# Cosine attention with a GELU layer: in batches 3 to 7, a score chunk issued in halves beside the values, sums of the third group later, and new run lengths

## The chip, the core and the metric

The kernel runs on one core of a Trainium2 chip. The metric is device time in microseconds (us): 401.73, the median of 3 runs (401.44 to 402.19). All other times come from one profiled execution; they are counted from the start of its span. Engines: TensorE (PE in the profile, PEld its weight loads), VectorE (DVE), ScalarE (ACT), GpSimd (POOL), and SP, which only issues transfers.

## The reference, cut to what matters

```python
# q, k, v: (8, 12, 448, 64); tau = 0.1; w_in: (768, 2048); w_out: (2048, 768)
q_n = q / (norm(q, axis=-1) + 1e-6);  k_n = k / (norm(k, axis=-1) + 1e-6)
attn = softmax(q_n @ k_n.T / tau)            # for each of 8 batches and 12 heads
x = (attn @ v) as (8 * 448, 12 * 64)         # heads side by side
out = gelu(x @ w_in) @ w_out                 # gelu with erf
```

The scores of normalised rows are at most 10, and the kernel leaves the maximum out of its softmax.

## The kernel before, in words

**Groups and chunks.** The 12 heads of a batch are three groups of four heads; there are 24 groups, `g0 = 3 * b` being a batch's first. A group's 448 keys are seven chunks of 64. `scores` (L232) computes one chunk for four heads as four 64x64 matmuls of 448 columns (a *quad* here): two on rows 0 to 63 of the array (s = 0), two on rows 64 to 127 (s = 1). The result fills a pair of PSUM banks; `exps` (L246) turns the pair into bf16 `pt` with one exp of 896 columns on ScalarE. `visit(p, ...)` (L647) does this for the next chunks in order, one for each number given, and the number says which of three bank pairs is used. The counter `at` runs ahead of the batch: the chunks that are scored in batch b >= 3 belong to a later group than the one whose values are taken.

**Values.** `values` (L317) multiplies a group's seven chunks by v, a quad each, into one more pair, `o`. `spread` (L355) lays out one over the softmax's sums, and `normalise` (L360) multiplies `o` by it into `x`, both on VectorE, twice a group. `weighted` (L371) is values, spread where that has not been done, and normalise.

**Sums.** From batch 3 on, the softmax's sums are not made by TensorE. A group's `pt` chunks are added up by GpSimd (`folded`, L258: the second and third group of a batch) or by VectorE (`gathered`, L265: the first). `turned_all` (L272) and `inverted_all` (L285) then reduce and invert them on VectorE (L276, L278, L281, L290, L294).

**Norms.** q and k are squared (L158), reduced (L168), and the root of each norm is taken by Ln and Exp on ScalarE (`norms`: L175, L180) and inverted on VectorE (`inverted_norms`: L186, L188). GpSimd scales q and k (L204), and SP's transfers transpose them (L216) for the scores.

**The two layers.** `first(b)` (L821) is x times w_in, 16 tiles `hp` of six matmuls each (L462), and GELU on ScalarE (L887). Four matmuls of each of the first six tiles come first, then the last two, which need the third group's part of `x`. The second layer, g times w_out (L399), is cut into *pieces* of 16 matmuls, each in one bank, which VectorE copies out (L403). The pieces of the batch before are the `fill` of `attention(b)`: 96 matmuls (batches 3, 5, 7) or 128 (batches 4, 6), which `run()` hands out in the lengths of `parts`, between the stretches of scores and values. So in batches 3 to 7 TensorE alternates between runs of op matmuls and stretches of quads.

**Banks.** Pieces and odd hp tiles share two banks, `mm0` and `mm1`; `mm_tile` takes the one whose turn it is and flips the turn. With `aside=0` it takes that bank and leaves the turn. Three more pairs serve scores, `o`, hp pairs (the dictionary `pairs` in `first`) and `gathered`.

**What sets the order.** The schedule is manual: each engine executes in the order in which the code issues, and waits for another engine where data or a buffer ask for it. VectorE's order therefore is the code's: a copy of a piece is issued with the piece's last matmul, and stands behind whatever was issued on VectorE before.

In batches 3 to 7 (the last branch of `attention`) the order before is: run, 3 visits around the first group's values, run, 3 visits, run, 3 visits around the second group's values, run, 3 visits, run, 3 visits with the norms and `turned_all` of the third group, run, the inversions, 3 visits, two runs, and 3 visits around the third group's values. In batch 7 only the chunks that are still left are scored.

```python
# L102 to L106
    def mm_tile(name, shape=(128, 512), dtype=F32, aside=None):
        t = ps_mm.tile(list(shape), dtype, tag=f"mm{turn[0] if aside is None else turn[0] ^ aside}", name=name)
        if aside is None:
            turn[0] ^= 1
        return t
```

Of the kernel before, what the change touches and what calls it, by code (L numbers as in the profile page):

```python
# [10 lines left out]
BF16 = mybir.dt.bfloat16  # L11
# [5 lines left out]
def kernel(  # L17
# [17 lines left out]
    nc = tc.nc  # L35
# [262 lines left out]
    def sums(g, chunks=range(C)):  # L298
        for c in chunks:
            if c == 0:  # L300
                bank_t[g, "sm"] = ps_acc.tile([128, 512], F32, tag="sm", name=f"sm{g}") if g < NQ else \
                    mm_tile(f"sm{g}", aside=0)
            for s in range(2):
                if g < NQ:
                    nc.tensor.matmul(bank_t[g, "sm"][64 * s:64 * (s + 1), :S],  # L305
                                     lhsT=ones2.rearrange("p a h r -> p (a h r)"), rhs=pt_t[g, s, c],
                                     start=(c == 0), stop=(c == C - 1), tile_position=(0, 64 * s))
                    continue

                half = 2  # L310
                for i in range(2) if c == half else ((c - (c > half)) % 2,):
                    r = 32 * (2 * s + i)
                    cols = slice(i * S // 2, (i + 1) * S // 2) if c == half else slice(0, S)
                    nc.tensor.matmul(bank_t[g, "sm"][r:r + 32, cols], lhsT=ones, rhs=pt_t[g, s, c][:, cols],  # L314
                                     start=(c < 2), stop=(c >= C - 2), tile_position=(0, r))

    def values(g, chunks=range(C), p=None):  # L317
        for c in chunks:
# [13 lines left out]
    rs_t = {}  # L332
# [314 lines left out]
    def visit(*pairs):  # L647
        for p in pairs:
            g, c = divmod(at[0], C)
            at[0] += 1  # L650
            if g < NG:
                scores(g, ((0, c), (1, c)), p)
                exps(g, ((0, c), (1, c)))

    def attention(b, fill):
        fill = list(fill)
        if b == 1:
            parts = iter((20, 13, 14, 17, 16, 16))
        elif b == 2:
            parts = iter((22, 12, 12, 13, 11, 13, 11, 11, 11, 6, 6))  # L660
        elif len(fill) == 128:
            parts = iter((20, 18, 18, 18, 18, 18, 9, 9))
        else:
            parts = iter((14, 13, 14, 14, 14, 13, 7, 7))

        def run(n=None):
            for _ in range(next(parts) if n is None else n):
                fill.pop(0)()

        def norms(n):  # L670
            if n < len(groups):
                logs(n)
                roots(n)
                done[root] = n + 1

        def inverted_norms(n):
            if n < len(groups):
                inverses(n)

        def squared(n, i):  # L680
            if n < NU:
                square(n, ((nc.scalar, i),))
                done[square] = n + 1

        def reduced(n, i):
            if n < NU:
                reduce(n, i)
                done[reduce] = n + 1

        x_t[b] = xp.tile([128, KD, S], BF16, tag="x", name=f"x{b}")  # L690
        g0, u = b * NQ, b * NQ + 1
        run()
        if b == 1:
            upto(scale, u + 3)
            upto(load_v, b + 2)
            upto(transposes, u + 3)
            upto(load_qk, g0 + NQ + 2)
            upto(square, u + 4)
            visit(0, 1, 2)
            run()  # L700
            visit(0, 1, 2)
            run()
            upto(load_qk, g0 + NQ + 3)
            visit(0, 1)
            upto(square, u + 5)
            run()
            visit(0, 1, 2)
            both(g0, 0)
            upto(load_v, b + 3)
            upto(load_qk, g0 + NQ + 4)  # L710
            visit(1, 2)
            upto(reduce, u + 4)
            run()
            visit(1, 2, 0)
            both(g0 + 1, 1)
            visit(2, 0)
            logs(6)
            roots(6)
            run()
            both(g0 + 2, 2)  # L720
            inverses(6)
            done[root] = 7
        elif b == 2:
            upto(scale, u + 3)
            upto(load_qk, g0 + 6)
            upto(transposes, u + 3)
            upto(scale, u + 4)
            upto(load_qk, g0 + 7)
            upto(transposes, u + 4)
            visit(0, 1, 2)  # L730
            run()
            visit(0, 1, 2)
            norms(9)
            inverted_norms(9)
            upto(scale, u + 5)
            upto(transposes, u + 5)
            upto(load_qk, g0 + 9)
            upto(square, u + 6)
            run()
            visit(1, 2)  # L740
            total(g0)
            weighted(g0, 0)
            visit(1, 2)
            squared(u + 6, 0)
            run()
            visit(1, 2, 0)
            run()
            reduced(u + 5, 0)
            visit(1, 2)
            squared(u + 6, 1)  # L750
            total(g0 + 1)
            weighted(g0 + 1, 0)
            visit(1, 2)
            reduced(u + 5, 1)
            folded(g0 + 2, range(C - 1))
            run()
            for i in range(2):
                reduced(u + 6, i)
            visit(1, 2, 0)
            folded(g0 + 2, range(C - 1, C))  # L760
            upto(load_v, b + 3)
            run()
            visit(1, 2, 0)
            run()
            visit(1, 2, 0)
            run()
            visit(1, 2, 0)
            norms(10)
            run()
            turned_all(g0 + 2)  # L770
            run()
            inverted_norms(10)
            inverted_all(g0 + 2)
            visit(1, 2)
            weighted(g0 + 2, 0)
            visit(1)
        else:
            upto(scale, u + 5)
            upto(transposes, u + 5)
            upto(load_qk, g0 + 9)  # L780
            visit(1, 2)
            weighted(g0, 0)
            visit(1)
            reduced(u + 5, 0)
            squared(u + 6, 0)
            folded(g0 + 2, range(3))
            run()
            reduced(u + 5, 1)
            visit(2, 1, 0)
            folded(g0 + 2, range(3, 6))  # L790
            run()
            reduced(u + 6, 0)
            for h in range(2):
                spread(g0 + 1, h)
            visit(2, 0)
            weighted(g0 + 1, 1)
            visit(2)
            squared(u + 6, 1)
            folded(g0 + 2, range(6, 7))
            upto(load_v, b + 3)  # L800
            run()
            visit(0, 2, 1)
            run()
            reduced(u + 6, 1)
            visit(0, 2, 1)
            norms(2 * b + 6)
            turned_all(g0 + 2)
            run()
            inverted_norms(2 * b + 6)
            inverted_all(g0 + 2)  # L810
            visit(0, 2, 1)
            run()
            run()
            for h in range(2):
                spread(g0 + 2, h)
            visit(1, 2)
            weighted(g0 + 2, 0)
            visit(1)
        assert not fill, len(fill)

    def first(b):  # L821
# [3 lines left out]
        nc.scalar.preload_act_table_set(GELU_SET)  # L825
        u = (b + 1) * NQ + 1
        hps = dict(early) if b == 0 else {}
        pairs = ({0: 1, 2: 0, 6: 1, 8: 0}, {2: 0, 4: 1, 6: 2, 8: 0}, {2: 2, 4: 1, 8: 2})[min(b, 2)]
        ahead = 6 if b else 5

        def mm(m, kds):
# [6 lines left out]
            elif m not in hps:  # L838
                hps[m] = mm_tile(f"hp{b}_{m}")[:, :S]

        for m in (0, 2, 3, 4, 5, 1) if b > 1 else range(ahead):
            bank(m)
            mm(m, range(2 if b == 0 and m in early else 0, KD - 2))
        if b == 0:
# [5 lines left out]
        elif b == 1:  # L850
            upto(scale, u + 1)
            upto(transposes, u + 1)
            upto(load_qk, (b + 1) * NQ + 5)
            upto(square, u + 3)
            upto(reduce, u + 2)
        elif b + 1 < B:
            for n in range(3, 5):
                upto(scale, u + n)
                upto(transposes, u + n)
                upto(load_qk, (b + 1) * NQ + 4 + n)  # L860
            folded((b + 1) * NQ + 1)
            if u + 4 < NU:
                square(u + 4, ((nc.scalar, 0), (nc.scalar, 1)))
            if u + 5 < NU:
                square(u + 5, ((nc.scalar, 0),))
            upto(reduce, u + 5)
            gathered((b + 1) * NQ, 0)
            turned_all((b + 1) * NQ)
            inverted_all((b + 1) * NQ)
            spread((b + 1) * NQ, 0)  # L870
            spread((b + 1) * NQ, 1)
            turned_all((b + 1) * NQ + 1)
            inverted_all((b + 1) * NQ + 1)
            done[square] = u + 6
# [94 lines left out]
```

## Time and profile before

| | |
|---|---|
| median of 3 runs | 401.73 us (401.44 to 402.19) |
| the profiled execution | 401.45 us, of which the span is 399.6 |
| granted TensorE clock | 1.000 |
| busy: PE, DVE, ACT, POOL | 98%, 66%, 67%, 63% of the span |
| hp matmuls L462 | 768, 147.0 us busy |
| op matmuls L399 | 864, 148.9 us busy |
| score matmuls L242 | 672, 49.5 us busy |
| value matmuls L328 | 672, 36.9 us busy |
| first hp matmul of batches 3, 4, 5, 6, 7 | 176.72, 225.24, 268.56, 317.08, 357.05 |
| exp over 896 columns L252 | 168, mean 916 ns |
| GELU over 448 columns L887 | 128, mean 552 ns |

How to read it: a line of the timeline gives start, length, engine, source line, operation, output and inputs, shapes, and how many instructions were merged; in square brackets stand the idle time before it and what ended that. Matmuls are pipelined, so their durations overlap, and the pace is read from their starts. An engine's idle time costs nothing unless TensorE waits for it in turn.

### The profile page before, as it was taken

How to read it: one execution, taken by the hardware profiler on the slowest of the kernel's cores; microseconds unless marked ns; L12 is line 12 of the kernel's file. 1: busy time of each engine (PE TensorE's matmuls, PEld its weight loads, DVE VectorE, ACT ScalarE, POOL GpSimd, SP SyncE). 2: the span in 40 equal slices, each digit the busy share in tenths (PEclk: the TensorE clock that was granted, in tenths of full speed). 3: DMA queues.
4: the chain of work that ended last, by engine and by line, in shares of the span. 5: the costliest groups of instructions: out<-in, count | busy, mean ns of one | idle time of the engine just before them, and what ended most of it. 6: DMA issues, size and time to landing. Idle time of an engine off the chain costs nothing.

```text
span 399.6 us, 8019 instructions
## 1 busy us (share of the span) xinstructions
PE 393.0 (98%) x3245; PEld 205.6 (51%) x3245; DVE 262.0 (66%) x530; ACT 266.9 (67%) x386; POOL 250.6 (63%) x162
## 2 busy tenths in 40 slices
PE   7999999999999999999999999999999999999996
PEld 3444555555545555555555555555555555555564
DVE  5787214955487999679976599679975695470021
ACT  6995787557998877797576867788656746504300
POOL 5898804269699694969495981969677760910000
PEclk9999999999999999999999999999999999999999
DMA  8999999847296890679066770665032700130033
GB/s 289 260 258 216 203 220 303 176 105 222 52 263 221 160 227 2 181 126 275 21 116 153 174 204 0 178 111 133 2 85 52 171 14 2 41 79 2 0 81 80
DMA packets 66485, 54.52 MB, mean 136 GB/s; under 512 B 38672, under 2 KB 62352, under 8 KB 66448
## 3 DMA queue, kind: packets, MB, share of 16 engines
q1 hardware_dynamic: 54464, 41.79, 39.5%
q0 software_dynamic: 11600, 11.80, 18.7%
q8 instruction: 25, 0.41, 0.4%
q10 hardware_dynamic: 384, 0.43, 0.4%
q14 instruction: 12, 0.10, 0.1%
HBM read 45.61 MB, written 11.01 MB: 142 GB/s over the span
## 4 chain that ended last, share of the span: by engine, by line
PE 95%; DMA 2%; SPq 1%; DVE 1%; ACT 1%; issue 0%; ACTq 0%
PE hp L462 37%; PE op L399 36%; PE st L242 10%; PE o L328 8%; DMA qk<-in_k_dram 2%; PE op L418 1%; PE sm L305 1%; PE sm L314 1%; PE tp L221 1%; SPq L133 1%; ACT sq L158 0%; PE spin L456 0%; ACT pt L252 0%; DVE tr L336 0%; DVE rs L357 0%
## 5 line engine op out<-in xcount | busy, mean ns | idle before, releaser
L252 ACT ACTIVATE pt<-st 128x896 bf16<-128x896 f32 x168 | 143.1, 916 | 37.0 <-PE st L242 36.5
L399 PE MATMUL op<-wo,g 128*128 128x384 bf16 x864 | 148.9, 327 | 0.0
L462 PE MATMUL hp<-x,wi 128*128 128x448 bf16 x768 | 147.0, 353 | 0.1
L204 POOL TENSOR_TENSOR qkb<-qk,rn 128x896 bf16<-128x896 f32 (+1 forms) x50 | 80.3, 1628 | 62.5 <-DVE rn L188 61.1
L399 PEld LDWEIGHTS <-g 128*128 128x128 bf16 x864 | 81.0, 98 | 64.7 <-issue 14.1
L462 PEld LDWEIGHTS <-wi 128*128 128x128 bf16 x768 | 74.4, 98 | 71.5 <-issue 3.1
L887 ACT ACTIVATE g<-hp 128x448 bf16<-128x448 f32 x128 | 63.6, 552 | 66.9 <-PE hp L462 66.7
L263 POOL TENSOR_TENSOR acc<-acc,pt 128x896 f32<-128x896 f32 x55 | 103.8, 1886 | 4.3
L403 DVE COPY ot<-op 128x384 f32<-128x384 f32 x54 | 29.6, 548 | 78.1 <-PE op L399 75.7
L168 DVE TENSOR_REDUCE nq<-sq 128x14 f32<-128x896 f32 (+1 forms) x50 | 50.9, 1038 | 12.8 <-POOL sq L160 6.7
L242 PE MATMUL st<-qkT 64*64 64x448 bf16 x672 | 49.5, 358 | 0.2 <-ACT pt L252 0.2
L160 POOL TENSOR_TENSOR sq<-qk 128x896 f32<-128x896 f32 x18 | 29.9, 1683 | 16.3 <-DMA qk<-in_q_dram 11.9
L328 PE MATMUL o<-pt,v 64*64 64x448 bf16 x672 | 36.9, 350 | 0.3 <-DVE x L362 0.3
L270 DVE TENSOR_TENSOR acc<-acc,pt 128x896 f32<-128x896 f32 x30 | 33.0, 1099 | 1.0
L362 DVE TENSOR_TENSOR x<-o,rs 128x448 bf16<-128x448 f32 x48 | 27.5, 608 | 9.1 <-PE o L328 8.8
L158 ACT ACTIVATE sq<-qk 128x896 f32<-128x896 f32 (+1 forms) x32 | 27.8, 899 | 2.4 <-DMA qk<-in_q_dram 1.9
L242 PEld LDWEIGHTS <-qkT 64*64 64x64 bf16 x672 | 16.7, 105 | 24.4 <-issue 18.2
L263 POOL TENSOR_TENSOR acc<-pt 128x896 f32<-128x896 bf16 x11 | 20.7, 1879 | 13.2 <-ACT pt L252 13.2
L357 DVE STREAM_TRANSPOSE rs<-rc 128x448 f32<-128x448 f32 x48 | 28.1, 621 | 0.4
L328 PEld LDWEIGHTS <-v 64*64 64x64 bf16 x672 | 19.1, 107 | 13.9 <-issue 3.1
L276 DVE STREAM_TRANSPOSE ta<-acc 128x448 f32<-128x448 f32 x32 | 18.6, 618 | 5.9 <-POOL acc L263 5.7
L278 DVE TENSOR_REDUCE sa<-ta 128x28 f32<-128x896 f32 x16 | 17.4, 1087 | 0.6
(49 smaller groups left out, 163.0 us busy)
## 6 DMA issues: line engine op xcount, KB each, us to landing
qk<-in_q_dram SPq DMA_DIRECT2D x23, 448.0 KB, 4.9
qk<-in_k_dram SPq DMA_DIRECT2D x23, 448.0 KB, 5.7
out_dram<-ot SPq DMA_DIRECT2D x48, 192.0 KB, 3.0
v<-in_v_dram POOLq DMA_DIRECT2D x7, 672.0 KB, 7.1
wo<-in_moe_w_out_dram POOLq DMA_DIRECT2D x4, 768.0 KB, 12.1
wi<-in_moe_w_in_dram POOLq DMA_DIRECT2D x4, 512.0 KB, 14.4
out_dram<-ot SPq DMA_DIRECT2D x12, 96.0 KB, 2.2
wi<-in_moe_w_in_dram POOLq DMA_DIRECT2D x4, 256.0 KB, 14.9
```

The lines of the kernel that those rows point to most:

```text
L160: eng.tensor_tensor(sq, t, t, ALU.mult)
L168: nc.vector.tensor_reduce(nq_t[n][:, j, i], sq_t[g, i][:, s0:s1], mybir.AxisListType.X, ALU.add)
L204: eng.tensor_tensor(qkb[:, i, :, s0:s1].rearrange("p c s d -> p s c d"), t[:, i, s0:s1], rn[:, i].to_broadcast([128, s1 - s0, C, D]), ALU. ...
L242: nc.tensor.matmul(st[cols, n, :S], lhsT=qkT[rows, 1, c, cols], rhs=qkT[rows, 0, :, cols], start=True, stop=True, tile_position=(64 * s, 6 ...
L252: nc.scalar.activation(pt, st[:, :, :S], AF.Exp, scale=inv_tau)
L263: nc.gpsimd.tensor_tensor(acc_t[g], all_t[g][:, 0] if c == 1 else acc_t[g], all_t[g][:, c], ALU.add)
L270: nc.vector.tensor_tensor(acc_t[g], acc_t[g], all_t[g][:, c], ALU.add)
L328: nc.tensor.matmul(bank_t[g, h][cols, :S], lhsT=v_t[g][rows, s, c, :], rhs=pt_t[g, s, c][rows], start=(c == 0), stop=(c == C - 1), tile_po ...
L399: nc.tensor.matmul(ps[:, :NH], lhsT=g_t[sb][:, kf, t * 128:(t + 1) * 128], rhs=wo[:, kf, ni * NH:(ni + 1) * NH], start=(kf == 0), stop=(kf ...
L403: nc.vector.tensor_copy(ot[:, ni * NH:(ni + 1) * NH], ps[:, :NH])
L462: nc.tensor.matmul(t, lhsT=wi[:, kd, m * 128:(m + 1) * 128], rhs=x_t[b][:, kd, :], start=(kd == 0), stop=(kd == KD - 1))
L887: nc.scalar.activation(g_t[sb][:, m, hf * S:(hf + 1) * S], hps.pop(m), AF.Gelu)
```

## The change

It touches batches 3 to 7 and the first layer after them.

- `mixed` takes the place of `weighted` for a group: one more score chunk is issued in two halves, each half in an `mm` bank with an exp of its own over 448 columns. The first half (s = 0, rows 0 to 63) is issued with the first two value matmuls of h = 1 (rows 64 to 127), the second half (s = 1) with the last two of h = 0; in between, the values of h = 0 of a chunk stand beside those of h = 1 of the next. One visit is put inside, two stand behind. Where no chunk is left to score, `mixed` is `weighted`.
- A batch then has six stretches of quads (11, 3, 11, 3, 3, 11); before it had seven. In batch 7 it is three (11, 10, 7) where it was four (10, 3, 8, 7).
- `parts` becomes (14, 22, 22, 26, 28, 8, 8) and (14, 17, 13, 18, 18, 8, 8): the first five add up to 112 and to 80, whole pieces.
- `turned_all` of the third group is issued behind the fifth stretch, with two runs of 8 and the last stretch to follow; its `spread` is issued behind the values.
- The last half score of a batch flips the turn of the `mm` banks.
- In `first`, the order of the first six hp tiles is 0 to 5 for all batches but 2, other pairs are used from batch 3 on, and `gathered` uses pair 1.

```diff
--- before.py
+++ after.py
@@ -313,6 +313,13 @@
                     cols = slice(i * S // 2, (i + 1) * S // 2) if c == half else slice(0, S)
                     nc.tensor.matmul(bank_t[g, "sm"][r:r + 32, cols], lhsT=ones, rhs=pt_t[g, s, c][:, cols],
                                      start=(c < 2), stop=(c >= C - 2), tile_position=(0, r))
+
+    def value(g, c, h):
+        rows = slice(64 * h, 64 * (h + 1))
+        for s in range(2):
+            nc.tensor.matmul(bank_t[g, h][64 * s:64 * (s + 1), :S], lhsT=v_t[g][rows, s, c, :],
+                             rhs=pt_t[g, s, c][rows], start=(c == 0), stop=(c == C - 1),
+                             tile_position=(64 * h, 64 * s))
 
     def values(g, chunks=range(C), p=None):
         for c in chunks:
@@ -652,6 +659,46 @@
                 scores(g, ((0, c), (1, c)), p)
                 exps(g, ((0, c), (1, c)))
 
+    def half_score(g, c, s, last):
+        qkT, rows = qkT_t[g], slice(64 * s, 64 * (s + 1))
+        st = mm_tile(f"sh{g}_{c}_{s}", aside=None if last else 0)
+        for h in range(2):
+            cols = slice(64 * h, 64 * (h + 1))
+            nc.tensor.matmul(st[cols, :S], lhsT=qkT[rows, 1, c, cols], rhs=qkT[rows, 0, :, cols],
+                             start=True, stop=True, tile_position=(64 * s, 64 * h))
+        return st
+
+    def half_exp(g, c, s, st):
+        pt_t[g, s, c] = all_t[g][:, c, s]
+        nc.scalar.activation(pt_t[g, s, c], st[:, :S], AF.Exp, scale=inv_tau)
+
+    def mixed(g, p, amid, behind, last=False):
+        q, c = divmod(at[0], C)
+        if q >= NG:
+            weighted(g, p)
+            return
+        at[0] += 1
+        if q not in all_t:
+            all_t[q] = ptp.tile([128, C, 2, S], BF16, tag="pt", name=f"pt{q}")
+        o = pair(p, f"o{g}")
+        bank_t[g, 0], bank_t[g, 1] = o[:, 0], o[:, 1]
+        st = half_score(q, c, 0, False)
+        value(g, 0, 1)
+        half_exp(q, c, 0, st)
+        for k in range(C - 1):
+            value(g, k, 0)
+            value(g, k + 1, 1)
+            if k == 0:
+                visit(*amid)
+        value(g, C - 1, 0)
+        st = half_score(q, c, 1, last)
+        half_exp(q, c, 1, st)
+        visit(*behind)
+        for h in range(2):
+            if (g, h) not in rs_t:
+                spread(g, h)
+            normalise(g, h)
+
     def attention(b, fill):
         fill = list(fill)
         if b == 1:
@@ -659,9 +706,9 @@
         elif b == 2:
             parts = iter((22, 12, 12, 13, 11, 13, 11, 11, 11, 6, 6))
         elif len(fill) == 128:
-            parts = iter((20, 18, 18, 18, 18, 18, 9, 9))
+            parts = iter((14, 22, 22, 26, 28, 8, 8))
         else:
-            parts = iter((14, 13, 14, 14, 14, 13, 7, 7))
+            parts = iter((14, 17, 13, 18, 18, 8, 8))
 
         def run(n=None):
             for _ in range(next(parts) if n is None else n):
@@ -778,44 +825,40 @@
             upto(scale, u + 5)
             upto(transposes, u + 5)
             upto(load_qk, g0 + 9)
-            visit(1, 2)
-            weighted(g0, 0)
-            visit(1)
+            mixed(g0, 0, (1,), (2, 1))
             reduced(u + 5, 0)
             squared(u + 6, 0)
             folded(g0 + 2, range(3))
             run()
             reduced(u + 5, 1)
-            visit(2, 1, 0)
-            folded(g0 + 2, range(3, 6))
-            run()
-            reduced(u + 6, 0)
             for h in range(2):
                 spread(g0 + 1, h)
-            visit(2, 0)
-            weighted(g0 + 1, 1)
-            visit(2)
+            if b + 1 < B:
+                visit(2, 0, 1)
+            else:
+                visit(2, 0)
+                weighted(g0 + 1, 1)
+                visit(2)
+            folded(g0 + 2, range(3, 6))
+            run()
+            reduced(u + 6, 0)
+            if b + 1 < B:
+                mixed(g0 + 1, 2, (0,), (1, 0))
             squared(u + 6, 1)
             folded(g0 + 2, range(6, 7))
             upto(load_v, b + 3)
             run()
-            visit(0, 2, 1)
-            run()
             reduced(u + 6, 1)
-            visit(0, 2, 1)
+            visit(1, 2, 0)
+            run()
+            visit(1, 2, 0)
             norms(2 * b + 6)
             turned_all(g0 + 2)
             run()
             inverted_norms(2 * b + 6)
             inverted_all(g0 + 2)
-            visit(0, 2, 1)
-            run()
-            run()
-            for h in range(2):
-                spread(g0 + 2, h)
-            visit(1, 2)
-            weighted(g0 + 2, 0)
-            visit(1)
+            run()
+            mixed(g0 + 2, 1, (2,), (0, 2), True)
         assert not fill, len(fill)
 
     def first(b):
@@ -825,7 +868,7 @@
         nc.scalar.preload_act_table_set(GELU_SET)
         u = (b + 1) * NQ + 1
         hps = dict(early) if b == 0 else {}
-        pairs = ({0: 1, 2: 0, 6: 1, 8: 0}, {2: 0, 4: 1, 6: 2, 8: 0}, {2: 2, 4: 1, 8: 2})[min(b, 2)]
+        pairs = ({0: 1, 2: 0, 6: 1, 8: 0}, {2: 0, 4: 1, 6: 2, 8: 0}, {2: 2, 4: 1, 8: 2}, {2: 0, 4: 2, 8: 0})[min(b, 3)]
         ahead = 6 if b else 5
 
         def mm(m, kds):
@@ -838,7 +881,7 @@
             elif m not in hps:
                 hps[m] = mm_tile(f"hp{b}_{m}")[:, :S]
 
-        for m in (0, 2, 3, 4, 5, 1) if b > 1 else range(ahead):
+        for m in (0, 2, 3, 4, 5, 1) if b == 2 else range(ahead):
             bank(m)
             mm(m, range(2 if b == 0 and m in early else 0, KD - 2))
         if b == 0:
@@ -864,7 +907,7 @@
             if u + 5 < NU:
                 square(u + 5, ((nc.scalar, 0),))
             upto(reduce, u + 5)
-            gathered((b + 1) * NQ, 0)
+            gathered((b + 1) * NQ, 0 if b < 3 else 1)
             turned_all((b + 1) * NQ)
             inverted_all((b + 1) * NQ)
             spread((b + 1) * NQ, 0)
```

More of the change, by code (lines that the diff above doesn't have):

```diff
@@ L788, in attention @@
             reduced(u + 5, 1)
-            visit(2, 1, 0)
+            for h in range(2):
+                spread(g0 + 1, h)
+            if b + 1 < B:
[4 more added lines that the diff above has]
+                visit(2)
             folded(g0 + 2, range(3, 6))
@@ L792, in attention @@
             reduced(u + 6, 0)
-            for h in range(2):
-                spread(g0 + 1, h)
-            visit(2, 0)
-            weighted(g0 + 1, 1)
-            visit(2)
+            if b + 1 < B:
+                mixed(g0 + 1, 2, (0,), (1, 0))
             squared(u + 6, 1)
@@ L801, in attention @@
             run()
-            visit(0, 2, 1)
+            reduced(u + 6, 1)
+            visit(1, 2, 0)
             run()
-            reduced(u + 6, 1)
-            visit(0, 2, 1)
+            visit(1, 2, 0)
             norms(2 * b + 6)
@@ L810, in attention @@
             inverted_all(g0 + 2)
-            visit(0, 2, 1)
             run()
-            run()
-            for h in range(2):
-                spread(g0 + 2, h)
-            visit(1, 2)
-            weighted(g0 + 2, 0)
-            visit(1)
+            mixed(g0 + 2, 1, (2,), (0, 2), True)
         assert not fill, len(fill)
```

## The prediction

> **What bounds the kernel now.** I read the page first: its second part, then the chain that ended last. TensorE is at 9 tenths in nearly every slice and carries the chain; no other engine holds more than 1% of it.
>
> ```profile
> PE   7999999999999999999999999999999999999996
> ...
> PE 95%; DMA 2%; SPq 1%; DVE 1%; ACT 1%; issue 0%; ACTq 0%
> ```
>
> The reader sees that time is gained only by shortening TensorE's own row, and lost wherever something makes TensorE wait. Next I read the timeline of TensorE alone for the stretches that change (batches 3 to 7, counted from 0). Batch 3 from its second half on:
>
> ```profile
> 169.41 2.29 PE L399 MATMUL op<-wo,g 128*128 128x384 bf16 x13
> 171.63 0.76 PE L242 MATMUL st<-qkT 64*64 64x448 bf16 x12
> 172.32 2.45 PE L399 MATMUL op<-wo,g 128*128 128x384 bf16 x14
> 174.70 0.57 PE L242 MATMUL st<-qkT 64*64 64x448 bf16 x8
> 175.10 1.49 PE L328 MATMUL o<-pt,v 64*64 64x448 bf16 x28
> 176.43 0.36 PE L242 MATMUL st<-qkT 64*64 64x448 bf16 x4
> ```
>
> Starts of single matmuls give the paces: op 0.1625 us each, hp 0.19, a quad of four 64x64 matmuls 0.189 (three score quads, 171.63 to 172.32: 0.69). From op to quads costs 0.094 extra, between the first two quads 0.024, from the last quad to op or hp 0.103: **0.22 us per round trip**. In batches 3 to 7 I find no other gap: TensorE waits for nobody there. So the change can win only round trips, and every wait that it makes is a loss. Third, VectorE's timeline at the end of the same batch:
>
> ```profile
> 171.84 1.17 DVE L276 STREAM_TRANSPOSE ta<-acc 128x448 f32<-128x448 f32 x2 [2.27 <-POOL acc L263]
> 173.04 1.08 DVE L278 TENSOR_REDUCE sa<-ta 128x28 f32<-128x896 f32 x1
> 174.16 0.73 DVE L281 TENSOR_REDUCE sa<-sa 32x28 f32<-32x28 f32 x4
> 174.93 0.56 DVE L403 COPY ot<-op 128x384 f32<-128x384 f32 x1
> 175.52 0.27 DVE L186 TENSOR_REDUCE se<-root 128x56 f32<-128x112 f32 x1
> 175.82 0.50 DVE L188 RECIPROCAL rn<-se 128x56 f32<-128x56 f32 x1
> 176.24 0.69 DVE L290 TENSOR_REDUCE su<-sa 64x14 f32<-64x28 f32 x4
> 176.97 0.33 DVE L294 RECIPROCAL rc<-su 128x28 f32<-128x28 f32 x1
> 177.22 0.49 DVE L403 COPY ot<-op 128x384 f32<-128x384 f32 x1
> 177.63 1.16 DVE L357 STREAM_TRANSPOSE rs<-rc 128x448 f32<-128x448 f32 x2
> ```
>
> This is the chain of sums. It starts when GpSimd's last add is done (171.80), and runs without a pause past 176.72, where hp begins. The copy of the batch's last op piece lands at 177.71, after hp has begun; that costs nothing now, since hp 0 sits in the bank of the piece before (copied by 175.5) and hp 1, which needs the late copy, comes sixth.
>
> **What it removes: five round trips.** Batches 3 to 6 have seven stretches of quads now (10, 3, 10, 3, 3, 3, 10 quads) and six then (11, 3, 11, 3, 3, 11); batch 7 four now, three then. The quads stay 42 a batch. 5 x 0.22 = **-1.10**. That the stretch of 11 runs at 0.189 a quad is not in the trace: one quad is now half score, half value, and value pairs keep to one half of the rows (0, 0, 64, 64, where values now alternate 0, 64, 0, 64). Score quads already issue 0, 0, 64, 64 and keep 0.189, so I take no cost. Below nothing is excluded, as the columns are the same; the upper end, halves that never run side by side, is 8 x 0.189 a stretch, 13 stretches: +19.7.
>
> The Trainium skill speaks against this order (TensorE: Matmul & The Clock Gate, Part 3): a weight load overlaps running matmuls only where the row group differs. By it one load of 0.107 us a quad could be exposed, 8 x 0.107 x 13 = 11 us; the score quads' row says none, and the row decides.
>
> **Half exps.** Each of the 13 new stretches has two exps of 448 columns for one of 896. Not in the trace; bounds are gelu over 448 columns (0.55 long, 0.435 from start to start in a row of four) and the exp over 896 (0.92 and 0.81). I take gelu's, being as wide; the other end adds 0.37 each. A score quad's exp can start 0.435 after the quad; an exp's end frees a bank for TensorE 0.05 later (107.481 to 107.533).
> - First stretch of a batch: 14 op matmuls, so two are left of piece 0, then piece 1 needs the second half score's bank. Its exp starts 1.537 + 0.435 after the stretch's first quad and ends at 2.52; with 0.05, 2.57. Piece 1 would start at 2.207 + 0.335 = 2.54. **+0.03 a batch, +0.15**; at the other bound +1.9.
> - Last stretch: ScalarE runs half, full, half, full, full, and the last exp ends 4.13 after the first quad, 1.9 after hp's natural start, against 1.04 now (226.28 to 225.24). GELU's table load, the squares, VectorE's reduces and its seven-add chain of the next batch follow one another, so **VectorE and GpSimd are 0.86 later into the next batch**, less whatever hp is held up itself.
>
> **The moved chain of sums.** It now stands behind the fifth stretch with 16 op matmuls and the last stretch ahead of hp. The program's order also moves two things: the flip of the last half score gives hp 0 the bank of the *last* op piece, and order 0, 1, 2.. makes hp 1 second. So hp cannot start before that copy. Costs from the rows above without the copy between: 1.20 + 1.12 + 0.77 to L186, 0.72 for the norms, 0.98 for L290 and L294, the copy 0.495, 0.05 to TensorE: **5.34 us from L276 to hp 0**.
> - Batch 3: GpSimd's adds hang on nothing that is moved, so L276 starts at 171.84 and hp at 177.18; natural start 176.72 - 0.22 + 0.03 = 176.53. **+0.65**.
> - Batches 4 and 6: adds are done early (batch 4: 215.0), the chain waits for the copy of the piece that ends the fourth run. From that run's last matmul: 0.37 to the copy, 0.47 to L276, 5.34: 6.18. TensorE: 0.16 + 0.09 + 0.70 + 2.70 + 2.21 = 5.86. **+0.32** in batch 4; in batch 6 only one norm group (0.49 for 0.72): **+0.09**.
> - Batch 5: L276 waits for GpSimd again (263.60 now), whose scales wait for VectorE's norms; these are 0.86 - 0.32 = 0.54 late beside a batch that begins 0.91 late. 263.60 + 1.45 + 5.34 = 270.39, against 268.56 now: the batch's shift grows from 0.91 to 1.83, which after -0.22 and +0.03 means **+1.11** of waits. (Some 0.3 may fall earlier, at the second value stretch, whose half score needs the copy of piece 1 behind two L357s.)
> - Batch 7: no norms; chain 0.37 + 0.47 + 4.07 + 0.55 = 5.46 behind piece 4; hp 1 is wanted after 0.16 + 2.70 + 1.45 + 0.76 = 5.07. **+0.39**.
>
> **The copy of piece 0 in batches 4 and 6.** With 20 matmuls before the first stretch VectorE copies piece 0 ahead of its two normalises; with 14 the copy stands behind them and L168. VectorE is free 4.97 after the first op (199.86 to 194.89). Batch 4, 0.21 to 0.24 late: 5.21 + 1.06 + 0.99 + 0.55 + 0.05 = 7.86; piece 2 needs that bank at 2.37 + 2.21 + 0.04 + 18 x 0.1625 = 7.54: **+0.32**. Batch 6, 0.05 late: **+0.13**. In batches 3 and 5 three quads come first and cover it.
>
> Transfers: the transposes and loads on SP behind scales move at most 3.6 us later (batch 4's norms, 220.1 to about 224), against more than 10 us until their use: nothing.
>
> **Sum:** -1.10 + 0.15 + 0.65 + 0.32 + 0.09 + 1.11 + 0.39 + 0.32 + 0.13 = **+2.06**. The profiled execution took 401.45 (span 399.6 and 1.85 around it): 403.5. The median of the three runs is 0.28 above it, so I say **403.6**.
>
> **Rivals.**
> 1. *Not slower: VectorE is in time.* If the chain of sums begins 0.65 us or more earlier than I count (before 171.2 in batch 3), and the lag of 0.86 is taken up, hp never waits, and 401.45 - 1.10 + 0.15 = 400.5 is left. For it: VectorE is busy only 66% and idles 2.27 ahead of L276. Against it: that idle ends with GpSimd's add, which is not moved.
> 2. *Level:* the waits in batches 3 and 5 alone, the lag being covered, so that batch 5 costs what batch 3 does: -1.10 + 0.15 + 2 x 0.65 = +0.35, 401.8.
> 3. *ScalarE binds:* half exps at the full price add 0.37 each: +1.9 at piece 1, and 0.4 or more of lag: about 405.8. For it: exps are ScalarE's costliest group. Against it: gelu's row.
> 4. *The halves do not run side by side:* from +4.9 (two quads of each stretch, 13 x 0.378) to +19.7: 408 to 423.
>
> **Chances.** Forecast (402.3 to 405.0) 0.66; rival 1, 0.08; rival 2 and the like, 0.12; rival 3, 0.10; rival 4, 0.04. The range 401.6 to 405.2 leaves out rival 1, rival 4 and the upper half of rival 3, and holds a little over 8 in 10. Within 0.2% (0.8 us) is about what a measurement can tell from no change: faster 0.08, same 0.12, slower 0.80.
>
> **What would show it.** Right: TensorE's list of waits names hp waiting for VectorE's copy of op in batches 3 to 7, longest in batch 5 (about 0.8 to 1.1), and op for the same copy early in batches 4 and 6; six stretches a batch with 11 quads in 2.2 us; L276 of batch 3 still at 171.84. Wrong: hp 0 starting with the last quad at its 0.29, or stretches of 11 quads over 2.4 us, or half exps over 0.6.

## The result, and the profile after

The changed kernel takes **403.41 us** (median) against 401.73: ratio 1.0042, 95% interval 1.0026 to 1.0058, so it is slower, by 0.4%. The profiled execution took 403.22 (span 401.5). The forecast was 403.6.

The page of the changed kernel, its slices of TensorE and its chain by engine:

```profile
PE   7999999999999999999999999999999999999996
...
PE 80%; DVE 10%; POOL 3%; ACT 2%; DMA 2%; issue 1%; SPq 1%; POOLq 0%; ACTq 0%
```

The slices look as before; waits of a few tenths of a us do not show in tenths of a 10 us slice. The chain tells more: a tenth of it now runs over VectorE, and some over GpSimd and ScalarE. Who made TensorE wait is one answer, the waits of TensorE from 150 us on (total, times, longest; the same answer for the kernel before is empty):

```profile
PE hp L469 <- DVE ot L410: 1.9, 4, 0.8
PE sh L667 <- DVE ot L410: 0.2, 1, 0.2
```

L410 is VectorE's copy of an op piece. The answer counts idle time only from a matmul's modelled end, and so misses short waits; below, waits are read from the starts of matmuls, as what a step takes over its usual pace. TensorE at the end of batch 3:

```profile
171.56 2.77 PE L406 MATMUL op<-wo,g 128*128 128x384 bf16 x16
174.26 0.38 PE L667 MATMUL sh<-qkT 64*64 64x448 bf16 x2
174.27 0.56 PE L320 MATMUL o<-pt,v 64*64 64x448 bf16 x6
174.66 0.36 PE L242 MATMUL st<-qkT 64*64 64x448 bf16 x4
174.85 1.30 PE L320 MATMUL o<-pt,v 64*64 64x448 bf16 x22
175.81 0.35 PE L667 MATMUL sh<-qkT 64*64 64x448 bf16 x2
175.99 0.55 PE L242 MATMUL st<-qkT 64*64 64x448 bf16 x8
177.11 1.11 PE L469 MATMUL hp<-x,wi 128*128 128x448 bf16 x5 [0.58 <-DVE ot L410]
```

The stretch of 11 quads runs from 174.26 to its last quad at 176.18; hp would follow 0.29 later, at 176.47, and starts at 177.11: a wait of 0.64, with its cause in the bracket. And VectorE in the same time:

```profile
171.78 1.17 DVE L276 STREAM_TRANSPOSE ta<-acc 128x448 f32<-128x448 f32 x2 [0.25 <-POOL acc L263]
172.99 1.09 DVE L278 TENSOR_REDUCE sa<-ta 128x28 f32<-128x896 f32 x1
174.11 0.73 DVE L281 TENSOR_REDUCE sa<-sa 32x28 f32<-32x28 f32 x4
174.87 0.27 DVE L186 TENSOR_REDUCE se<-root 128x56 f32<-128x112 f32 x1
175.17 0.50 DVE L188 RECIPROCAL rn<-se 128x56 f32<-128x56 f32 x1
175.59 0.69 DVE L290 TENSOR_REDUCE su<-sa 64x14 f32<-64x28 f32 x4
176.32 0.33 DVE L294 RECIPROCAL rc<-su 128x28 f32<-128x28 f32 x1
176.57 0.49 DVE L410 COPY ot<-op 128x384 f32<-128x384 f32 x1
```

The piece was complete at about 174.4 (0.37 behind its last matmul's start); its copy starts at 176.57, as the last of the chain, and ends 0.05 before hp's start.

All waits of batches 3 to 7, from starts of matmuls (us). The first hp matmul of batch 2 and the last matmul of the kernel are the yardstick of the last row: between them lies all that was changed, while the time to the former, in code that no kernel here changes, differed by up to 1.2 us from one execution to another (133.28 to 134.51).

| | forecast | after |
|---|---|---|
| five round trips | -1.10 | -1.18 |
| half exp ahead of piece 1, five batches | +0.15 | +0.13 |
| ahead of hp 0, batch 3 | +0.65 | +0.64 |
| ahead of hp 0, batch 4 | +0.32 | +0.30 |
| batch 5: second value stretch, and ahead of hp 0 | +1.11 | +0.30 and +0.86 |
| ahead of hp 0, batch 6 | +0.09 | +0.07 |
| ahead of hp 1, batch 7 | +0.39 | +0.44 |
| piece 2, batches 4 and 6 | +0.32, +0.13 | +0.29, +0.08 |
| sum | +2.06 | +1.93 |
| first hp of batch 2 to the last matmul | | 262.61 to 264.49: +1.88 |

The round trips' -1.18 is 5 x 0.236, taken from the second experiment below, where almost nothing else is left; read from the starts of matmuls a round trip costs 0.23. The sum of all waits and round trips is 0.05 above the yardstick.

### The profile page after: what moved, and what is told of

Its sections match the earlier page's. It is cut to its first block, busy times and chain, and to the rows that moved or that the text cites. A ratio compares the mean times of both kernels' runs of the same rounds, so it can differ in the third digit from the quotient of the medians.

```text
span 401.5 us, 8027 instructions
## 1 busy us (share of the span) xinstructions
PE 392.2 (98%) x3245; PEld 208.2 (52%) x3245; DVE 262.7 (65%) x530; ACT 267.7 (67%) x399; POOL 250.5 (62%) x162
## 4 chain that ended last, share of the span: by engine, by line
PE 80%; DVE 10%; POOL 3%; ACT 2%; DMA 2%; issue 1%; SPq 1%; POOLq 0%; ACTq 0%
PE hp L469 32%; PE op L406 30%; PE st L242 7%; PE o L335 3%; PE o L320 3%; POOL acc L263 3%; DMA qk<-in_k_dram 2%; DVE acc L270 2%; DVE ta L276 1%; DVE sa L278 1%; PE op L425 1%; PE sm L305 1%; ACT pt L252 1%; PE sm L314 1%; DVE sa L281 1%
## 5 line engine op out<-in xcount | busy, mean ns | idle before, releaser
L252 ACT ACTIVATE pt<-st 128x896 bf16<-128x896 f32 x155 | 132.5, 916 | 29.4 <-PE st L242 29.0
L410 DVE COPY ot<-op 128x384 f32<-128x384 f32 x54 | 29.5, 547 | 77.8 <-PE op L406 75.7
L242 PE MATMUL st<-qkT 64*64 64x448 bf16 x620 | 46.0, 356 | 0.2 <-ACT pt L252 0.2
L242 PEld LDWEIGHTS <-qkT 64*64 64x64 bf16 x620 | 18.0, 105 | 20.5 <-issue 12.9
L320 PE MATMUL o<-pt,v 64*64 64x448 bf16 x364 | 24.2, 351 | 0.0
L673 ACT ACTIVATE pt<-sh 128x448 bf16<-128x448 f32 x26 | 14.1, 544 | 9.5 <-PE sh L667 8.8
L276 DVE STREAM_TRANSPOSE ta<-acc 128x448 f32<-128x448 f32 x32 | 18.5, 617 | 0.9 <-POOL acc L263 0.7
L335 PE MATMUL o<-pt,v 64*64 64x448 bf16 x308 | 17.5, 351 | 0.5 <-DVE x L369 0.5
```

The source lines that it names most:

```text
L242: nc.tensor.matmul(st[cols, n, :S], lhsT=qkT[rows, 1, c, cols], rhs=qkT[rows, 0, :, cols], start=True, stop=True, tile_position=(64 * s, 6 ...
L252: nc.scalar.activation(pt, st[:, :, :S], AF.Exp, scale=inv_tau)
L320: nc.tensor.matmul(bank_t[g, h][64 * s:64 * (s + 1), :S], lhsT=v_t[g][rows, s, c, :], rhs=pt_t[g, s, c][rows], start=(c == 0), stop=(c == ...
L335: nc.tensor.matmul(bank_t[g, h][cols, :S], lhsT=v_t[g][rows, s, c, :], rhs=pt_t[g, s, c][rows], start=(c == 0), stop=(c == C - 1), tile_po ...
```

## The experiments

My theory: VectorE's copies come late, for two reasons that feed each other. At the end of a batch the copy of the last piece stands behind the chain of sums. At the beginning VectorE is late because ScalarE's exps of the last stretch end later; a wait ahead of hp hides that lag, and without it the lag comes out at the next batch. The rival: the waits at the end of the batch, or the new bank order, are the whole loss. The yardstick, from the first hp matmul of batch 2 to the last matmul, is 262.61 before and 264.49 after. Ratios are to the kernel before, which took 402.07 beside the first four experiments and 402.33 beside the last three, against 401.73 in the result. So the times of the first four came out up to 0.4 above what I expected; as differences from the kernel before they lie within 0.1 of it.

**The copy ahead of the inversions.**

```diff
             turned_all(g0 + 2)
             run()
+            run()
             inverted_norms(2 * b + 6)
             inverted_all(g0 + 2)
-            run()
             mixed(g0 + 2, 1, (2,), (0, 2), True)
```

> The changed kernel, with the two inversions of the third group and of the norms issued behind the second run of 8, so that the last op piece is copied ahead of them. My theory: hp no longer waits (the 2.3 us of waits ahead of hp 0 and hp 1 go), but VectorE then is the full 0.86 late into the next batch, so the wait of piece 2 in batches 4 and 6 grows from 0.29 and 0.08 to about 0.9 each and that of batch 5's second value stretch from 0.30 to about 0.6: only about 0.3 us better than the changed kernel, 403.0 to 403.2. Rival: the waits ahead of hp are the whole cost and nothing comes back: 401.1.

Measured: 403.26, ratio 1.0038 (1.0004 to 1.0071), yardstick 264.00. hp waits nowhere. TensorE's waits from 150 us on:

```profile
PE op L406 <- DVE ot L410: 1.5, 2, 0.8
PE sh L667 <- DVE ot L410: 0.4, 1, 0.4
```

From the starts: piece 2 waits 0.92 in batch 4 and 0.92 in batch 6, and batch 5 waits 0.14 and 0.47. So 2.31 us of waits ahead of hp are gone and 0.5 us of time; the rest came back a batch later. The rival falls.

**Three moves.** The edit above, and:

```diff
             mixed(g0, 0, (1,), (2, 1))
-            reduced(u + 5, 0)
             squared(u + 6, 0)
             folded(g0 + 2, range(3))
             run()
+            reduced(u + 5, 0)
             reduced(u + 5, 1)
-            for h in range(2):
-                spread(g0 + 1, h)
+            if b + 1 == B:
+                for h in range(2):
+                    spread(g0 + 1, h)
```

> The first experiment's edit, and besides it the first reduce of norms moved behind the second run and the second group's spreads left to the end of its own stretch, so that the copies of pieces 0 and 1 stand two instructions earlier on VectorE. My theory: all waits but the 0.03 a batch behind the half exp go, and the five round trips are gained: 400.5, 2.7 to 2.9 us below the changed kernel and 0.9 to 1.0 below the one before. Rival (the stretch of 11 quads or its half exps cost something that the waits hide): 401.5 or more.

Measured: 400.92, ratio 0.998 (0.9941 to 1.0019), yardstick 261.56: 1.05 below before, 2.93 below after. The answer on TensorE's waits from 150 us on is empty; from the starts only the 0.03 a batch ahead of piece 1 is left. VectorE at the end of batch 3:

```profile
174.65 0.73 DVE L281 TENSOR_REDUCE sa<-sa 32x28 f32<-32x28 f32 x4
175.42 0.56 DVE L410 COPY ot<-op 128x384 f32<-128x384 f32 x1
176.00 0.27 DVE L186 TENSOR_REDUCE se<-root 128x56 f32<-128x112 f32 x1
```

The copy ends at 175.98, and hp starts at 177.01, 0.29 behind the last quad. So neither the stretch of 11 quads nor its half exps hide a cost of their own: with the waits gone the round trips remain, (1.05 + 0.13) / 5 = 0.236 each. Run once more for its time:

> The second experiment's kernel once more, for its time against the kernel before: its first interval reached across no change. My theory: 0.997 to 0.998 of the kernel before, about 400.6. Rival: no difference that holds (0.999 to 1.001).

Measured: 401.11 against 402.33, ratio 0.9962 (0.9932 to 0.9993), yardstick 261.58. The first interval reached across no change, this one does not. By the yardstick, twice the same within 0.02, this version gains 1.0 us on the kernel before, a quarter of a per cent, and both intervals hold that.

**The bank order of before.**

```diff
-            mixed(g0 + 2, 1, (2,), (0, 2), True)
+            mixed(g0 + 2, 1, (2,), (0, 2))
...
-        for m in (0, 2, 3, 4, 5, 1) if b == 2 else range(ahead):
+        for m in (0, 2, 3, 4, 5, 1) if b >= 2 else range(ahead):
```

> The changed kernel, with the bank order of before at the end of a batch: the last half score does not flip the turn, and the first six hp tiles go 0, 2, 3, 4, 5, 1. hp 0 then sits in the half score's bank and waits for its exp, hp 1 comes sixth. My theory: about 0.36 a batch ahead of hp in batches 3 to 6 (exp over at 2.57, hp due at 2.21) in place of 0.64, 0.30, 0.86, 0.07, and no wait in batch 7; a shorter wait ahead of hp leaves more lag to the next batch: 402.7 to 403.3. Rival: the flip alone makes the loss: 401.3.

Measured: 403.57, ratio 1.0032 (1.0008 to 1.0056), yardstick 264.40. TensorE's waits from 150 us on:

```profile
PE hp L469 <- ACT pt L673: 1.2, 4, 0.3
PE op L406 <- DVE ot L410: 0.7, 2, 0.4
```

hp now waits for the half score's exp, 0.36 in each of batches 3 to 6 and 0.05 more at the next tile, piece 2 waits 0.53 and 0.52, and batch 5's second value stretch 0.20. The flip changes which engine TensorE waits for, not what it loses.

**The reduce and the spreads alone**, the second diff without the first.

> The changed kernel with the second part of the second experiment alone (first reduce behind the run, spreads of the second group left to its stretch); the inversions stay ahead of the last copy. My theory: the waits of piece 2 (0.29 and 0.08) go; the 0.30 of batch 5's second stretch goes too but comes back ahead of hp, where the chain of sums decides: 402.9 to 403.1. Rival (reduce and spreads are what holds TensorE up, the sums only pass it on): 401.5.

Measured: 403.23, ratio 1.0036 (1.0006 to 1.0065), yardstick 264.15. The waits of piece 2 and of batch 5's second stretch are gone, and hp waits 0.66, 0.30, 1.17, 0.07 and (hp 1) 0.44: in batch 5 the 0.30 has moved from the second stretch to hp (0.86 to 1.17), where the chain of sums decides. The gain is 0.34; the rival, at 401.5, asked for about 1.9.

**Eight matmuls from the fifth run to the last.**

```diff
-            parts = iter((14, 22, 22, 26, 28, 8, 8))
+            parts = iter((14, 22, 22, 26, 20, 8, 16))
-            parts = iter((14, 17, 13, 18, 18, 8, 8))
+            parts = iter((14, 17, 13, 18, 10, 8, 16))
```

> The changed kernel with 8 op matmuls moved from the fifth run to the last one, so that the fifth stretch no longer stands at a full piece and the chain of sums has 24 op matmuls ahead of hp in place of 16. My theory: in batches 4 and 6 the chain starts earlier and the wait ahead of hp (0.30, 0.07) goes; in batches 3 and 5 GpSimd's last add still sets the chain's start, and the copy of a piece now falls into the chain, so that the waits grow from 0.64 and 0.86 to about 1.1 and 1.3; in all 0.2 to 0.4 above the changed kernel. Rival (the chain merely has too little work behind it, 8 matmuls more cure it): all waits ahead of hp gone, 1.5 us and more below the changed kernel.

Measured: 406.1, ratio 1.0101 (1.0064 to 1.0138), yardstick 266.65: 2.16 above the changed kernel, where I had said 0.2 to 0.4. The rival falls, but my sum was wrong too. TensorE's waits from 150 us on:

```profile
PE sh L667 <- DVE ot L410: 2.5, 3, 1.1
PE op L406 <- DVE ot L410: 1.5, 2, 0.8
```

VectorE at the end of batch 3 shows the first reason:

```profile
172.49 1.17 DVE L276 STREAM_TRANSPOSE ta<-acc 128x448 f32<-128x448 f32 x2 [2.85 <-POOL acc L263]
173.69 1.09 DVE L278 TENSOR_REDUCE sa<-ta 128x28 f32<-128x896 f32 x1
174.81 0.73 DVE L281 TENSOR_REDUCE sa<-sa 32x28 f32<-32x28 f32 x4
175.58 0.56 DVE L410 COPY ot<-op 128x384 f32<-128x384 f32 x1
```

With the fifth stretch in the middle of a piece, the copy of the piece *before* the last stands in the chain as well, and the last stretch's first half score needs that piece's bank: it waits 1.00 in batch 3 and 1.22 in batch 5, ahead of the stretch instead of behind it. I had looked only at hp's bank. Ahead of hp nothing waits any more. The second reason is the lag again: the exps of the last stretch move with it, nothing hides their lateness, and piece 2 waits 0.91 in batches 4 and 6, batch 5's second stretch 0.47 and a piece before it 0.14. A smaller third one: in batches 3 and 5 the fourth and fifth stretches stand only 10 op matmuls apart, and a score quad waits 0.18 for a pair that ScalarE's exp has not yet read (the exp ends at 170.82, the quad starts at 170.87). In the changed kernel the fifth run's end at a full piece is what keeps that copy ahead of the chain.

**The lag itself.** The first experiment's edit, and one visit of the last stretch moved between the two runs of 8:

```diff
-            visit(1, 2, 0)
+            visit(2, 1, 0)
             norms(2 * b + 6)
             turned_all(g0 + 2)
             run()
+            visit(2)
             run()
             inverted_norms(2 * b + 6)
             inverted_all(g0 + 2)
-            mixed(g0 + 2, 1, (2,), (0, 2), True)
+            mixed(g0 + 2, 1, (0,), (2,), True)
```

> The first experiment (copy ahead of the inversions) with one visit of the last stretch moved between the two runs of 8. It costs one round trip more in four batches (0.9 us) and takes one exp of 0.81 from what ScalarE has to do when hp begins. My theory: VectorE's lag into the next batch comes from ScalarE's exps, so the wait of piece 2 in batches 4 and 6 falls from 0.92 to about 0.1 and the waits of batch 5 (0.47 and 0.14) go; 1.2 us below the first experiment from the first hp of batch 2 to the last matmul, about 0.2 above the kernel before. Rival (VectorE is late by its own spreads and normalises, which stand behind the values): the waits stay and the round trips come on top, 0.9 above the first experiment.

Measured: 402.16, ratio 0.9992 (0.9966 to 1.0018), yardstick 263.11: 0.89 below the first experiment, where I had said 1.2, and 0.50 above before, which the ratio cannot tell from no change. Piece 2 waits 0.30 and 0.32, batch 5 nothing. ScalarE at the end of batch 3, first in the changed kernel, then here:

```profile
176.68 1.72 ACT L252 ACTIVATE pt<-st 128x896 bf16<-128x896 f32 x2
178.42 1.28 ACT L868 ACT_TABLE_LOAD   x1
179.71 2.63 ACT L158 ACTIVATE sq<-qk 128x896 f32<-128x896 f32 x3
```

```profile
177.93 0.91 ACT L252 ACTIVATE pt<-st 128x896 bf16<-128x896 f32 x1
178.86 1.28 ACT L869 ACT_TABLE_LOAD   x1
```

The last exp ends 1.31 behind hp's start here (178.84 to 177.53), 1.93 in the first experiment, 1.04 before; VectorE's first reduce of squares starts 3.60, 4.22 and 3.33 behind hp. The two go together to 0.01. On VectorE that reduce follows the spreads and normalises of the last stretch. In the changed kernel and here:

```profile
180.69 2.08 DVE L168 TENSOR_REDUCE nq<-sq 128x14 f32<-128x896 f32 x2 [1.15 <-ACT sq L158]
```

```profile
181.14 2.08 DVE L168 TENSOR_REDUCE nq<-sq 128x14 f32<-128x896 f32 x2 [0.43 <-ACT sq L158]
```

VectorE is done with its own work and idle until ScalarE's squares come, so the lag is ScalarE's, and the rival falls. The lag shrank by 0.62 against the first experiment, and the wait of piece 2 by 0.60 to 0.62. The remainder of 0.27, which leaves that wait at 0.30 and not at 0.1, I had missed: the stretch, now 10 quads, is shorter, but its half exps are still two, and the last exp (177.93) stands behind the second of them (177.49).

## Why the prediction was right, step by step

- *Only round trips can be won, and every wait is a loss.* Held: with the waits away (three moves) the round trips and the 0.03 a batch are left. A round trip is worth 0.236, not 0.22: the first op matmul behind a stretch is slower by 0.01 too, and the last 0.005 I cannot place.
- *Quads of one score half and one value half run at 0.189.* Held: the 11 quads of batch 3 take 174.26 to 176.18, 0.189 each and 0.02 at the first. The Trainium skill's rule that a weight load overlaps running matmuls only where the row group differs (TensorE: Matmul & The Clock Gate, Part 3) would have cost up to 11 us here by the prediction's estimate; the 0.189 a quad shows no part of it.
- *Half exps priced by GELU's row.* Held: 0.544 long, 0.44 from one to the next exp; the wait ahead of piece 1 was 0.025 to 0.027 where 0.03 was forecast.
- *Last piece's copy behind the chain of sums, 5.34 from L276 to hp 0.* Held: 171.78 to 177.11 is 5.33.
- *GpSimd sets the chain's start in batch 3, the end of the fourth long run in batches 4 and 6.* (The fourth long run is the fifth of the batch's runs.) Held: 171.78 against 171.84 forecast, and a wait of 0.30 against 0.32. In batch 5 the forecast of 1.11 measured 0.30 + 0.86, of which the 0.30 at the second value stretch had been named; L276 starts there 0.56 later behind batch 4's first hp than before (264.92 - 226.00 against 263.60 - 225.24), where 0.54 was forecast.
- *VectorE 0.86 late into the next batch, less what hp itself waits.* Held, and the first experiment shows it bare: the last exp ends 0.89 later behind hp than before (1.93 against 1.04), and piece 2 waits 0.92, where 0.94 follows from the prediction's terms for piece 0 (4.97 + 0.86 + 1.06 + 0.99 + 0.55 + 0.05 - 7.54). This step was argued in the prediction; the first and the sixth edit turned it into a measurement.
- *Transfers cost nothing.* Held: no wait for a transfer shows on TensorE. The transposes behind batch 4's norms start 2.9 and 3.1 us later (225.12 to 228.00, 228.20 to 231.30), within the 3.6 forecast.
- Misses, all small: the round trips (-1.10, measured -1.18), batch 5 (1.11, measured 1.16), hp 1 in batch 7 (0.39, measured 0.44) and piece 2 in batch 6 (0.13, measured 0.08). They have both signs; that the sum misses the waits by only 0.13, and the yardstick by 0.18, is in part luck.
- *From the sum to 403.6.* Wrong by its own terms: 401.45 + 2.06 is 403.5, and with the 0.28 between the median and the profiled execution 403.8, not 403.6. That 403.6 lies nearer to the measured 403.41 is luck too.
- *The sign in the list of waits.* Half of it came: hp waits for the copy of op, longest in batch 5, but op is not on the list early in batches 4 and 6. Those waits of 0.29 and 0.08 show only in the starts of matmuls.

The rivals: "not slower" needed a chain that starts before 171.2; it started at 171.78. "Level" needed the lag to be covered; piece 2 waited. ScalarE did not bind at the full price, and the halves ran side by side.

## What to carry to other kernels

Where an engine empties the banks that TensorE writes, its queue is part of TensorE's path: count what is issued ahead of each copy, at the place where the copy is issued, before merging stretches of matmuls. A wait that is taken away shows its value only behind the next place that the same late engine serves: here 2.3 us of waits gave back 0.5. The 1 us of the change was to be had by three moves in VectorE's and the code's order, none of which touched TensorE's.

## What the runs showed of the hardware that I had not expected

- The change from 128x128 to 64x64 matmuls and back costs 0.23 us by the starts (0.236 as a fifth of what three moves left), the same within 0.01 whether 3, 10 or 11 quads lie between. That is small, but in batches 3 to 7 of the kernel before no other gap shows between TensorE's matmuls.
- Executions of the same code up to the first hp matmul of batch 2 ended between 133.28 and 134.51 us, a spread wider than the 1.05 us that three moves gain. Between two fixed instructions of the trace the two profiles of that kernel agree within 0.02 us, so differences of 0.1 us can be read there, which medians of runs do not show.
